# Moving the first norm's statistics to the head of each stage in a fused convolution and feed-forward kernel

## The chip, the cores and the metric

The kernel runs on one core of a Trainium2 chip, in one launch. The core has five engines with queues of their own: TensorE (PE, with its weight loads PEld), VectorE (DVE), ScalarE (ACT), GpSimd (POOL) and SyncE (SP, which here issues nearly all transfers). The metric is the device time of one execution in microseconds; the median of the shown runs is compared. Before the change it is 531.88 us (five runs, 529.43 to 533.68).

## The reference

One block of a diffusion-style network works on 2048 rows (tokens) of 576 channels in bfloat16. Six modulation vectors come from a condition vector. The rows `x` (called `A_q` among the inputs) go through a norm, a gated long convolution and a residual, then through a second norm, a gated feed-forward layer and a second residual.

```
sa, ca, ga, sb, cb, gb = six rows of 576 from silu(c) @ w_mod
h  = layernorm(x) * (1 + ca) + sa
kv = (4-tap shifted sum of k) * v
y  = causal convolution of kv with ssm_k (2048 taps per channel) + kv * ssm_D
x  = x + ga * (h * y)
h  = layernorm(x) * (1 + cb) + sb
x  = x + gb * ((silu(h @ w1) * (h @ w3)) @ w2)     # 576 -> 4608 -> 576
```

The change touches where the statistics of the first `layernorm` are computed, so that line and the product `h * y` are what matters here.

## The kernel before

**Tiling.** The rows are cut into 8 blocks of 256 (two rows to a partition, so a block is a tile of 128 x 2 x 576). The long convolution is done block by block with a short transform: each block of `kv` becomes a spectrum `X` and each block of the filter a spectrum `V`, both by matmuls with a small basis (`L299`, `L313`), which ACT copies out of PSUM (`L302`, `L315`). The spectra are multiplied and summed on DVE (`pair`: `L407`, `L412`, `L414`, 3456 elements to a partition each). `real_parts` (`L516` to `L523`) and `inverse` (PE, `L536`) bring the sum back, ACT copies it to `y` (`L737`), and `residual` (`L550`, `L551`) multiplies by the normed rows `hg` and adds to `x`. Then come the second norm's statistics, its rows `h2row`, a transposition on PE (`L568`) and five ACT instructions that write `h2T` (`L598`), the input of the feed-forward layer.

**The feed-forward layer** runs over 4 row blocks of 512 rows, two convolution blocks each. `stream` makes the hidden part item by item (matmuls `L902` and, for the last 64 channels, `L913`; ACT `sg` L920 and `u` L922; DVE product `h` L924), `down` the second matmul (`L965`) with weights `w2t`. PSUM has four buffers of two banks, shared by the feed-forward items and by the convolution's matmuls.

**Stages.** The convolution of the blocks that row block r + 1 will need is done while row block r is computed. `first_block` does block 0 alone; `conv_second` does block 1 beside the first 12 half-wide items; then `conv(2)` (blocks 2 and 3) runs beside row block 0, `conv(4)` beside row block 1, `conv(6)` beside row block 2. Row block 3 has nothing beside it.

**What sets the order.** The convolution functions are generators. Each `yield` names a cost in us; `advance`, called after each feed-forward item and each chunk of `down`, takes as many steps as their costs allow, so a step's cost moves all that comes after it. `mix` lays steps of a second generator into the gaps that negative costs leave; the four numbers handed to `outcome` are such gaps. The program so written is then put into queues by a scheduler with priorities, which may shift instructions by some places on each engine; where the text below says that one instruction stands behind another, it is by the built programs. Each engine takes its queue in order. `behind(engine)` ties a group to its place after the last instruction so far of that engine.

**The first norm.** `ln_sums` is two ACT instructions for one of a tile's two rows, a sum and a sum of squares (`L442`, output `junk`), `ln_stats` does both rows, and `ln_scales` is six small POOL instructions (`L457` to `L462`), which give scale `l1r` and bias `l1n`. `gate_rows` is two ACT instructions that write the normed rows `hg` (`L497`), and `gate` two DVE instructions that put the modulation on them (`L508`, `L510`). Before the change each block's statistics are taken at one stroke: block 1's at the start of `conv_second`, the first block's of a pair at the head of `conv`, the second block's (`s1`) not until the first block's outcome is under way.

**Loads.** `load_x` brings a block of `x` (288 KB), `load_kv` one of `k` and `v` (720 and 288 KB), `load_k` one of the filter; all are issued by SP in program order among the weights `wst` and `w2t`. `x` has four buffers, `k` and `v` one each.

Of the kernel before, what the change touches and what calls it, by code (L numbers as in the profile page):

```python
# [10 lines left out]
F32 = mybir.dt.float32  # L11
# [4 lines left out]
P = 128  # L16
# [27 lines left out]
class _Kernel:  # L44
    def __init__(self, ctx, tc, q, k, v, shift_k, ssm_k, ssm_D, w1, w3, w2, c, w_mod, out):
        self.tc, self.nc = tc, tc.nc
        self.q, self.k, self.v = q, k, v
        self.shift_k, self.ssm_k, self.ssm_D = shift_k, ssm_k, ssm_D
        self.w1, self.w3, self.w2, self.c, self.w_mod, self.out = w1, w3, w2, c, w_mod, out
        pool = lambda name, **kw: ctx.enter_context(tc.tile_pool(name=name, **kw))  # L50
        self.const = pool("const", bufs=1)
        self.psum = pool("psum", bufs=4, space=bass.MemoryType.PSUM)
        self.dram = pool("spill", bufs=1, space=bass.MemoryType.DRAM)
        self.spec = pool("spec", bufs=4)
        self.wprev = pool("wprev", bufs=2)
        self.prod = pool("prod", bufs=1)
        self.acc = pool("acc", bufs=1)
        self.ld = pool("ld", bufs=1)
        self.kvp = pool("kvp", bufs=1)
        self.x1p = pool("x1p", bufs=4)  # L60
        self.lnp = pool("lnp", bufs=1)
        self.small = pool("small", bufs=4)
        self.hp = pool("hp", bufs=2)
        self.w2p = pool("w2p", bufs=NW2)
        self.xo, self.hg, self.accs = {}, {}, {}
        self.X, self.V, self.Wl = {}, {}, {}
        self.n_w13, self.w13, self.kept = 0, {}, {}

# [415 lines left out]
        return self.tc.issue_after(last)  # L484

    def gate_stats(self, s):
        with self.behind(self.nc.scalar):
            self.l1 = self.ln_stats(self.xo[s], "l1")

    def gate_rows(self, s):  # L490

        x1 = self.xo[s]
        r, b = self.l1
        hg = self.lnp.tile([P, 2, D], BF16, name="hg", tag="hg")
        with self.behind(self.nc.scalar):
            for i in range(2):
                self.nc.scalar.activation(hg[:, i, :], x1[:, i, :], ACT.Identity, bias=b[:, i:i + 1],  # L497
                                          scale=r[:, i:i + 1])
        self.hg[s] = hg
# [267 lines left out]
        self.turned(s, pt, 0, 2)  # L767

    def conv_second(self):
        self.gate_stats(1)  # L770
        yield from self.kv_rows(1)
        yield from self.v_block(1)
        yield from self.pair(self.X[0], self.V[1], 1)
        self.gate_rows(1)
        yield from self.gate(1)
        yield from self.x_spectrum(1)
        self.mod_piece(5)
        self.load_k(2)
        yield from self.x_sums(1)
        yield from self.pair(self.X[1], self.V[0], 1)  # L780
        self.load_kv(2)
        yield from self.outcome(1, self.mix(self.filter_ahead(2)), (3.5, 3.5, 0.0, 2.0), quick=True)
        self.turn_all(1)
        yield 0.0

    def conv(self, s0):
        s1 = s0 + 1
        if s0 == 2:
            self.load_k(s1)
        self.load_x(s0)  # L790
        self.load_x(s1)

        def filters():
            yield from self.k_rows(s1)
            yield -4.0
            yield from self.v_block(s0)
            yield from self.w_spectrum(s1)

        def old():
            V, X = self.old_v(s0 - 1, s0), self.old_x(1, s0)  # L800
            yield from self.pair(X, V, s0)
            for j in range(2, s0):
                X = self.old_x(j, s0)
                yield from self.pair(X, V, s1)
                V = self.old_v(s0 - j, s0)
                yield from self.pair(X, V, s0)
            self.V1 = V
            self.gate_stats(s0)
            yield from self.kv_rows(s0)
            if s0 == 2:  # L810
                yield from self.pair(self.X[0], self.V[s0], s0)
        yield from self.mix(filters(), old())
        self.gate_rows(s0)
        X0, V0 = self.old_x(0, s0), self.old_v(0, s0)

        def beside():
            yield from self.v_block(s1)
            if s0 > 2:
                yield from self.pair(X0, self.V[s0], s0)
            self.X1 = self.old_x(1, s0)  # L820
            yield from self.pair(X0, self.V[s1], s1)
            yield from self.gate(s0)
        yield from self.mix(self.x_spectrum(s0), beside())
        yield from self.x_sums(s0)
        yield from self.pair(self.X[s0], V0, s0)

        def more():
            yield from self.pair(self.X1, self.V[s0], s1)
            yield from self.pair(self.X[s0], self.V1, s1)

        def others():
            self.gate_stats(s1)
            yield from self.kv_rows(s1)
            yield from self.mix(self.x_spectrum(s1), more())
            yield from self.x_sums(s1)
        yield from self.outcome(s0, others(), (5.0, 4.5, 6.0, 0.0), lambda: self.gate_rows(s1))
        yield from self.pair(self.X[s1], V0, s1)
        yield from self.gate(s1)
        ahead = self.mix(self.filter_ahead(s1 + 1)) if s1 + 1 < NBLK else ()
        yield from self.outcome(s1, ahead, (3.5, 3.5, 4.0, 4.0), lambda: self.turn_all(s0))  # L840
        self.turn_all(s1)
        yield 0.0
# [244 lines left out]
```

## Time and profile before

The profiled execution took 533.68 us; its span from the first to the last instruction is 532.0 us, with a mean granted TensorE clock of 0.981.

| engine | busy us | share of the span | instructions |
|---|---|---|---|
| PE | 501.4 | 94% | 3324 |
| PEld | 294.8 | 55% | 3351 |
| DVE | 340.9 | 64% | 515 |
| ACT | 292.8 | 55% | 581 |
| POOL | 71.8 | 13% | 109 |

| stretch of the span, us | what runs |
|---|---|
| 0 to 34 | block 0 alone |
| 34 to 76 | 12 half-wide items, block 1 beside them |
| 76 to 183 | row block 0, blocks 2 and 3 beside it |
| 183 to 303 | row block 1, blocks 4 and 5 beside it |
| 303 to 421 | row block 2, blocks 6 and 7 beside it |
| 421 to 532 | row block 3 |

PE is the busiest engine nearly everywhere, but a share of busy time does not tell where PE waits: for that the stretches and the waits are to be read one by one. In rows of the timeline the first number is the start in us from the span's start, the second how long it lasted, and the square bracket at the end is the engine's idle time before it with what ended it. A row that ends in "x4" merges four instructions in a row.

### The profile page before, as it was taken

Reading aid. Unit: us, or ns where it says so; the run is one execution under the profiler, and the core shown is the slowest. Engines: PE = TensorE matmul, PEld = TensorE weight load, DVE = VectorE, ACT = ScalarE, POOL = GpSimd, SP = SyncE. Lnnn points to the kernel's source line nnn. Section 1 sums busy time; section 2 is a strip of 40 time slices with the busy share of each in tenths; the row PEclk is TensorE's granted clock in tenths of the full one; section 3 lists DMA queues with packets and bytes.
Section 4 is the critical chain, followed back from the end, with each engine's and each line's share of the span. In section 5 each row is a group of like instructions: output and inputs, shape, how many; then the busy total and the mean of one; then the engine's idle time right before and its main releaser. Section 6 shows DMA issues by size and latency. Waiting matters only on the chain.

```text
span 532.0 us, 8687 instructions
## 1 busy us (share of the span) xinstructions
PE 501.4 (94%) x3324; PEld 294.8 (55%) x3351; DVE 340.9 (64%) x515; ACT 292.8 (55%) x581; POOL 71.8 (13%) x109
## 2 busy tenths in 40 slices
PE   7896989997998999999999999999999999999997
PEld 3664865453875743434577643344577644444775
DVE  8897987997992417599997799269772121121011
ACT  6665689558543067757927065776825255455000
POOL 3313001093020000007201000000511000000000
PEclk9988999997997999999999999999999999999999
DMA  8957599673974874378999984464555544541462
GB/s 273 339 163 227 159 287 289 192 256 89 293 229 156 272 264 153 115 229 317 281 350 329 364 254 134 148 200 142 168 157 134 156 128 150 169 127 53 112 174 72
DMA packets 102205, 107.77 MB, mean 203 GB/s; under 512 B 5075, under 2 KB 94228, under 8 KB 102164
## 3 DMA queue, kind: packets, MB, share of 16 engines
q1 hardware_dynamic: 102142, 107.21, 64.4%
q8 instruction: 26, 0.43, 0.3%
q14 instruction: 15, 0.12, 0.1%
q10 hardware_dynamic: 22, 0.01, 0.0%
HBM read 96.00 MB, written 11.21 MB: 202 GB/s over the span
## 4 chain that ended last, share of the span: by engine, by line
PE 66%; DVE 12%; ACT 9%; POOL 5%; DMA 4%; issue 2%; SPq 0%; POOLq 0%; ACTq 0%; DVEq 0%
PE ps L902 35%; PE ps L965 21%; PE ps L913 5%; POOL l1m L457 3%; DVE p L412 3%; DVE z L414 2%; ACT junk L442 2%; DMA wst<-in_B_w_dram 2%; PE ps L313 2%; DVE h L924 1%; ACT h2T L598 1%; DMA V<-Vd 1%; PE ps L536 1%; ACT hg L497 1%; DMA knat<-in_A_ssm_k_dram 1%
## 5 line engine op out<-in xcount | busy, mean ns | idle before, releaser
L902 PE MATMUL ps<-h2T,wst 128*128 128x512 bf16 (+1 forms) x1317 | 267.0, 352 | 5.5 <-DMA wst<-in_B_w_dram 1.9
L902 PEld LDWEIGHTS <-wst 128*128 128x128 bf16 x1344 | 128.6, 99 | 126.9 <-issue 20.8
L920 ACT ACTIVATE sg<-ps 128x512 bf16<-128x512 f32 x144 | 86.3, 599 | 136.7 <-PE ps L913 92.7
L965 PE MATMUL ps<-w2t,h 128*128 128x288 bf16 x1152 | 147.1, 289 | 1.0 <-DMA w2t<-in_B_w_dram 0.8
L965 PEld LDWEIGHTS <-h 128*128 128x128 bf16 x1152 | 113.5, 99 | 31.2 <-issue 1.4
L924 DVE TENSOR_TENSOR h<-sg,u 128x512 bf16<-128x512 bf16 x144 | 60.7, 424 | 95.1 <-ACT u L922 95.0
L922 ACT CAST u<-ps 128x512 bf16<-128x512 f32 x144 | 84.2, 585 | 0.9 <-DVE h L924 0.9
L412 DVE TENSOR_TENSOR p<-X,V 128x3456 bf16<-128x3456 bf16 x28 | 54.8, 1957 | 16.9 <-DMA X<-Xd 11.5
L414 DVE TENSOR_TENSOR z<-z,p 128x3456 bf16<-128x3456 bf16 x28 | 54.8, 1957 | 0.1
L457 POOL TENSOR_SCALAR l1m<-l1s 128x2 f32<-128x2 f32 x7 | 26.3, 3759 | 203.2 <-ACT junk L442 203.2
L913 PE MATMUL ps<-h2T,wst 64*128 64x512 bf16 (+1 forms) x336 | 42.8, 351 | 3.7 <-ACT X L315 3.7
L979 DVE TENSOR_TENSOR og<-ps,gbrow 128x288 bf16<-128x288 f32 x32 | 13.3, 452 | 51.1 <-PE ps L965 51.1
L442 ACT ACTIVATE junk<-x 128x576 bf16<-128x576 bf16 x54 | 37.3, 691 | 0.4
L913 PEld LDWEIGHTS <-wst 64*128 64x128 bf16 x336 | 11.4, 94 | 31.3 <-issue 28.3
L598 ACT ACTIVATE h2T<-ps,sbcol,cbcol 128x256 bf16<-128x256 bf16 x35 | 16.7, 568 | 10.8 <-PE ps L568 10.8
L563 ACT ACTIVATE h2row<-x,l2n,l2r 128x576 bf16<-128x576 bf16 (+1 forms) x24 | 13.7, 642 | 10.7 <-POOL l2n L462 10.7
L335 DVE TENSOR_TENSOR kv<-kv,kvt 128x1152 bf16<-128x1152 bf16 x24 | 18.2, 757 | 0.2
L334 DVE TENSOR_TENSOR kvt<-kh,shk 128x1152 bf16<-128x1152 bf16 x24 | 18.2, 757 | 0.2
L737 ACT CAST y<-ps 128x576 bf16<-128x576 f32 x14 | 8.4, 653 | 16.7 <-PE ps L536 16.7
L315 ACT CAST X<-ps 128x576 bf16<-128x576 f32 x24 | 15.7, 653 | 1.0 <-PE ps L313 1.0
L497 ACT ACTIVATE hg<-x,l1n,l1r 128x576 bf16<-128x576 bf16 x14 | 11.4, 867 | 6.9 <-POOL l1n L462 6.9
L457 POOL TENSOR_SCALAR l2m<-l2s 128x2 f32<-128x2 f32 x6 | 3.5, 579 | 86.0 <-ACT junk L442 86.0
(136 smaller groups left out, 361.2 us busy)
## 6 DMA issues: line engine op xcount, KB each, us to landing
wst<-in_B_w_dram SPq DMA_DIRECT2D x80, 512.0 KB, 4.9
w2t<-in_B_w_dram SPq DMA_DIRECT2D x72, 288.0 KB, 3.8
X<-Xd SPq DMA_DIRECT2D x8, 864.0 KB, 7.6
Xd<-X SPq DMA_DIRECT2D x6, 864.0 KB, 5.2
wst<-in_B_w_dram SPq DMA_DIRECT2D x80, 64.0 KB, 2.2
kh<-in_A_k_dram SPq DMA_DIRECT2D x7, 720.0 KB, 6.0
Vd<-V SPq DMA_DIRECT2D x4, 864.0 KB
V<-Vd SPq DMA_DIRECT2D x4, 864.0 KB, 5.3
```

The costliest lines, as they stand in the source:

```text
L334: nc.vector.tensor_mul(tmp[:], kh[:, 3 - j:5 - j, :], tap(j))
L412: nc.vector.tensor_mul(p[:], X[:], V[:])
L414: nc.vector.tensor_add(z[:], z[:], p[:])
L442: self.nc.scalar.activation(junk[:], src[:, i, :], func, accum_out=out[:, col:col + 1])
L457: e.tensor_single_scalar(mean[:], ssum[:], -1.0 / D, op=ALU.mult)
L598: nc.scalar.activation(dst, src, ACT.Identity, bias=self.sbcol[:, ct:ct + 1], scale=self.cbcol[:, ct:ct + 1])
L902: nc.tensor.matmul(gus[k][:, i, a * n:(a + 1) * n], w[:, 5 * i + ct, (fi + a) * P:(fi + a + 1) * P], hT[:, ct, t0:t1], start=(first and ct ...
L913: nc.tensor.matmul(gus[k][:, i, a * n:(a + 1) * n], w[rows, 4, (fi + a) * P:(fi + a + 1) * P], hT[rows, 4, t0:t1], start=(first and a == 0 ...
L920: nc.scalar.activation(sg[:], gus[k][:, 0, :], ACT.Silu)
L922: nc.scalar.copy(u[:], gus[k][:, 1, :])
L924: nc.vector.tensor_mul(self.h3[:, f:f + m, t0:t1], sg[:].rearrange("p (a t) -> p a t", a=m), u[:].rearrange("p (a t) -> p a t", a=m))
L965: nc.tensor.matmul(acc[t], self.h3[:, f0 + f, t * P:(t + 1) * P], w[:, f, :], start=(f0 + f == 0), stop=(f0 + f == NF - 1))
```

## The change

The statistics are taken row by row, with a cost of 0.8 after each row, and kept in a table by block. In `conv_second` they follow `v_block(1)`, and `gate_rows(1)` and `gate(1)` move from ahead of block 1's spectrum to behind it and behind `mod_piece(5)` (ten matmuls and an ACT copy). In `conv` the second block's statistics move from `others` to just behind `kv_rows(s0)`, so both blocks' statistics stand ahead of `gate_rows(s0)`. The loads of `x` for blocks 2 and 3 move from the head of `conv(2)` into `conv_second`, ahead of `load_kv(2)`, and the first gap of block 1's `outcome` is 5.0 rather than 3.5.

```diff
     def gate_stats(self, s):
-        with self.behind(self.nc.scalar):
-            self.l1 = self.ln_stats(self.xo[s], "l1")
+        ssum, ssq = [self.small.tile([P, 2], F32, name="l1" + k, tag=t) for k, t in (("s", "ssum"), ("q", "ssq"))]
+        for i in range(2):
+            with self.behind(self.nc.scalar):
+                self.ln_sums(self.xo[s], i, ssum, ssq)
+            yield 0.8
+        self.l1[s] = self.ln_scales(ssum, ssq, "l1")
...
     def gate_rows(self, s):
         x1 = self.xo[s]
-        r, b = self.l1
+        r, b = self.l1.pop(s)
...
     def conv_second(self):
-        self.gate_stats(1)
         yield from self.kv_rows(1)
         yield from self.v_block(1)
+        yield from self.gate_stats(1)
         yield from self.pair(self.X[0], self.V[1], 1)
+        yield from self.x_spectrum(1)
+        self.mod_piece(5)
         self.gate_rows(1)
         yield from self.gate(1)
-        yield from self.x_spectrum(1)
-        self.mod_piece(5)
         self.load_k(2)
         yield from self.x_sums(1)
         yield from self.pair(self.X[1], self.V[0], 1)
+        self.load_x(2)
+        self.load_x(3)
         self.load_kv(2)
-        yield from self.outcome(1, self.mix(self.filter_ahead(2)), (3.5, 3.5, 0.0, 2.0), quick=True)
+        yield from self.outcome(1, self.mix(self.filter_ahead(2)), (5.0, 3.5, 0.0, 2.0), quick=True)
...
     def conv(self, s0):
         s1 = s0 + 1
         if s0 == 2:
             self.load_k(s1)
-        self.load_x(s0)
-        self.load_x(s1)
+        else:
+            self.load_x(s0)
+            self.load_x(s1)
...
             self.V1 = V
-            self.gate_stats(s0)
+            yield from self.gate_stats(s0)
             yield from self.kv_rows(s0)
+            yield from self.gate_stats(s1)
             if s0 == 2:
                 yield from self.pair(self.X[0], self.V[s0], s0)
...
         def others():
-            self.gate_stats(s1)
             yield from self.kv_rows(s1)
             yield from self.mix(self.x_spectrum(s1), more())
             yield from self.x_sums(s1)
```

## The prediction

> **What bounds the kernel now.** I read the page's slices first, then busy time by stretches of 10 us, then PE's waits, then the timeline around each. PE is 9.95 of 10 us busy in most stretches; its loss sits in a few places, and there the clock falls too.
>
> ```profile
> 40.00:50.00 10.00, 5.59 (x41) 3.77 (x39) 6.87 (x11) 6.38 (x12) 4.73 (x6) 0.93 0.93 296
> 120.00:130.00 10.00, 6.29 (x23) 2.57 (x21) 6.59 (x11) 8.25 (x18) 4.47 (x10) 0.69 0.21 61
> 160.00:170.00 10.00, 7.87 (x46) 5.46 (x47) 3.56 (x10) 4.67 (x9) 0.73 (x2) 0.66 0.46 149
> 210.00:220.00 10.00, 9.95 (x52) 4.00 (x52) 4.11 (x9) 9.09 (x20) 1.71 (x6) 1.00 0.48 144
> 240.00:250.00 10.00, 9.66 (x52) 4.35 (x52) 9.85 (x12) 8.15 (x18) 8.61 (x3) 1.00 0.94 322
> ```
>
> Columns: PE, PEld, DVE, ACT, POOL busy us (instructions), granted clock, DMA share and GB/s. The clock is halved for 3.41 us from 48.67 and for 6.83 us from 123.76 and from 161.31, each time after a gap in PE; at half rate these cost 1.7, 3.4 and 3.4 us. The middle one has this cause:
>
> ```profile
> 106.85 12.94 POOL L457 TENSOR_SCALAR l1m<-l1s 128x2 f32<-128x2 f32 x1 [23.29 <-ACT junk L442]
> ...
> 119.28 0.44 DVE L924 TENSOR_TENSOR h<-sg,u 128x512 bf16<-128x512 bf16 x1
> ...
> 121.61 1.62 ACT L497 ACTIVATE hg<-x,l1n,l1r 128x576 bf16<-128x576 bf16 x2 [4.32 <-POOL l1n L462]
> ...
> 123.27 0.76 DVE L508 TENSOR_TENSOR hg<-hg,arow 128x1152 bf16<-128x1152 bf16 x1 [3.55 <-ACT hg L497]
> ...
> 124.47 0.61 PE L913 MATMUL ps<-h2T,wst 64*128 64x512 bf16 x2 [3.71 <-ACT X L315]
> ```
>
> Block 3's POOL chain starts at 106.85, while DVE runs without a pause; an instruction that elsewhere takes 0.22 us ends at 119.79, when DVE has run dry (119.72) because it waits for the same rows. ACT's queue stands behind `hg`, so no PSUM buffer comes free and PE stops for 3.71 us. Two other gaps matter:
>
> ```profile
> 43.80 1.63 PE L299 MATMUL ps<-kv,Fb 128*128 128x288 bf16 x12 [2.12 <-DVE kv L337]
> ...
> 47.72 0.65 PE L299 MATMUL ps<-kv,Fb 128*128 128x288 bf16 x4 [2.29 <-ACT u L922]
> ...
> 161.76 0.72 PE L568 MATMUL ps<-ident,h2row 128*128 128x128 bf16 x5 [2.66 <-ACT h2row L563]
> ```
>
> The second is block 1's `hg` blocking ACT's `u`; the third is the end of block 3: DVE is 95 to 100% busy from 90 to 163 but for that one idle of 3.55 us, so this end is set by DVE and the chain behind it.
>
> **Part 1, block 1.** PE's wait of 2.12 stays: `kv` L337 ends at 43.65 in either order. With `hg` behind the four X copies and `gbrow`, the wait of 2.29 shrinks to about 0.4 and the half-clock window goes: some 3.6 us. But DVE then idles from 43.65 to about 48.0, since the X copies stand behind the four L442 (0.82 each, start to start), and the work that it did meanwhile is still to do: from its X sums to block 1's last `h2row` it took 49.89 to 68.87, 19.0 us with 1.1 idle; now 48.0 + 17.9 + five L508/L510/L334/L335-like instructions of 0.75 = 69.7, and 71.3 with the POOL waits and `h` products that fall between. The turn L568 now stands behind the 12th item instead of before it, so its cover is gone: 71.5 + 0.73 + the five `h2T` at 0.47 to 0.57, which the next item consumes one by one, ends that item at 75.8, against 75.4. **+0.4** (-2 to +2): what PE gains first it loses at the turn. The transfers: two `x` of 288 KB now stand on SP ahead of `k`, `v` (both wait for `kv_rows(1)`, to 43.65) and of the next weights (44.12); at 340 GB/s they take 1.7 us of DMA, and those weights, landing 4.9 us after issue, are needed at about 52. Nothing, or up to 1 us if late.
>
> **Part 2, blocks 2 and 3.** ACT is 9.96 of 10 us busy from 80 to 90, and there block 3's four L442 now stand, ahead of `hg` of block 2: 3.3 us. By place: `u` of items 14, 15, 16 come 1.3, 2.2 and 3.4 us later, the last filter copy `Wo` over 4. PE runs out of PSUM buffers at about 84.5 and waits 2.2 us for item 15's. DVE, behind `Wo` and `u`, ends its third L407 (91.91 before) at about 96.4 when one more `h` is taken off: 4.5 late. It had 3.42 us of idle there (before 82.93), which the filter work moved behind block 1 and this lag eat.
>
> POOL's two chains then run in DVE's pauses at 82 to 88 at 0.2 to 0.7 us an instruction, and block 3's `hg` has its scales 35 us early. So DVE gets the 3.55 back: +1.0 at block 3. PE gets its 3.71 and the half-clock back, yet meets DVE earlier: about 3 us at `kv` L337 of block 3 (it waited 1.21 there) and again at block 2's inverse. The end is DVE's. From there, `h2row` of block 3 comes at -0.3 to +1.0, I take **+0.5**. The turn now has 128 matmuls L965 behind it rather than 144: 16 x 0.1225 = **-2.0**. And PE arrives at it about 1.5 us before the rows rather than 2.97 (weight load), so the window at 161.31 should go: **-3.4**. Part 2: -4.9; -1.5 with that window kept.
>
> [...] By this trace a gap of 2.29 us inside one stretch of 3.41 us (45.26 to 48.67) halved the next stretch; 1.96 us of a stretch (41.84 to 45.26) did not. [...] The measured row decides; I take no window at 84.5, by the length nearest to 1.96.
>
> [...]
>
> **Part 3, blocks 4 to 7.** The same four L442 now stand right ahead of `hg` of blocks 4 and 6 (ACT 9.09 of 10 at 210 to 220), two items later than before, by the 0.8 costs. ACT then owes 1.6 for `hg` and 3.3 for the L442; counting PSUM buffers as above PE waits 0.6 + 0.7 = **+1.3** at 222 and about **+1.0** in row block 2, where an X copy falls between. Nothing comes back: block 5's L457 took 7.59 us (240 to 250) and PE was 9.66 busy. Bounds 0 to +2.5 each. DVE's later start (2 to 4 us) is met by PE's turns, which also stand 16 to 32 L965 later.
>
> **Sum.** +0.4 lies inside part 2's absolute times. -4.9 + 1.3 + 1.0 = -2.6 on a span of 532.0, that is 529.4 (533.68 with what lies around it becomes 531.1). The profiled run was the slowest of five; against the median 531.88 - 2.6 = **529.3**.
>
> **Rivals.**
> - *The stall comes back whole* (525.3): ACT's extra work fits into DVE's 3.42 idle, DVE is not late, and the turn comes 3.55 earlier: -3.55 - 2.0 - 3.4 + 2.3 = -6.6. For it: that idle. Against it: ACT at 9.96.
> - *The window at the turn stays* (532.7): -1.5 + 2.3 = +0.8. For it: the turn still waits.
> - *Slower, DVE falls behind at 84 to 92* (535.2): the gap at 84.5 halves the clock, items come at half pace for 3.4 us or more, and DVE's lag is 7 rather than 4.5. With the window at the turn kept: 7 - 4.0 - 2.0 + 2.3 = +3.3. It decides from a lag of 3.7 us with that window, 7.1 without. For it: 2.2 is close to 2.29.
> - *The change does not do what it says* (536.7): DVE pauses too little at 86 to 88, POOL is held until block 3's rows are wanted, and the stall recurs on top of the lag: 4.5 - 2.0 + 2.3 = +4.8. Against it: DVE waits there for `Wo` and `u`.
>
> **How the numbers follow.** Chances: forecast 0.36 (own range 527 to 532), stall back whole 0.18, window stays 0.17, DVE behind 0.21, POOL held 0.08. 0.5% is 2.7 us, about what a measurement of this kernel tells from no change. Faster: 0.18 + 0.6 of 0.36 = 0.40. Slower: 0.29 + a sixth of 0.17 + a little of the forecast's = 0.33. Same 0.27. The range 524.5 to 536.5 leaves out the outer part of the first and last rivals and the bounds of part 3 beyond them.
>
> **What would show it.** Right: block 3's L457 under 1 us near 86; no gap of 3.7 before an L913 near 120; a gap of 2 us near 85 and one of 3 at block 3's L313; the clock at 1.00 from 165 to 180; gaps of about 1 us near 222 and 340. Wrong: a half-clock window after 85, a POOL instruction of over 10 us, or DVE idle between 90 and 160.

## The result, and the profile after

The changed kernel takes 530.62 us in the median of 43 runs (526.96 to 534.76), the kernel before 531.62 us in 80 runs beside it: ratio 0.9985, 95% interval 0.9971 to 0.9999. It is about 1 us faster, less than the 0.5% that the forecast called measurable, where 2.6 us were forecast. Its profiled execution took 529.5 us with a span of 527.4 us and a clock of 0.994; that of before had 533.68, 532.0 and 0.981. So the two spans lie 4.5 us apart and the medians 1.0. Most of what follows is about that difference.

In the changed file the lines below the change stand 5 to 8 further down: L902 is L910, L913 L921, L922 L930, L924 L932, L965 L973, L979 L987, L497 L502, L508 L513, L568 L573.

The same stretches of 10 us (columns: PE, PEld, DVE, ACT, POOL busy us, granted clock, DMA share, GB/s):

```profile
40.00:50.00 10.00, 8.22 (x76) 5.95 (x75) 7.03 (x9) 8.96 (x19) 1.72 (x6) 1.00 1.06 350
80.00:90.00 10.00, 7.98 (x53) 4.29 (x51) 4.72 (x9) 10.00 (x24) 3.81 (x12) 1.00 0.91 298
120.00:130.00 10.00, 9.19 (x69) 5.53 (x66) 9.96 (x16) 9.32 (x21) 3.78 (x6) 1.00 0.44 137
160.00:170.00 10.00, 10.00 (x84) 7.98 (x83) 4.25 (x4) 2.39 (x5) 0.00 (x0) 1.00 0.82 264
210.00:220.00 10.00, 9.04 (x47) 3.80 (x47) 3.92 (x8) 9.62 (x20) 1.71 (x6) 1.00 0.38 117
```

The stall at 120 is gone (PE 9.19 instead of 6.29), and the clock is whole in all five. At 80 to 90 ACT is full and PE at 7.98, which is the price that the forecast named; before, the same stretch reads:

```profile
80.00:90.00 10.00, 9.84 (x70) 5.97 (x71) 6.92 (x13) 9.96 (x22) 1.72 (x6) 1.00 0.84 253
```

From the timeline of the changed kernel:

```profile
84.47 0.22 POOL L457 TENSOR_SCALAR l1m<-l1s 128x2 f32<-128x2 f32 x1 [1.90 <-ACT junk L442]
...
84.91 1.46 PE L910 MATMUL ps<-h2T,wst 128*128 128x512 bf16 x5 [1.89 <-ACT u L930]
...
92.59 1.95 DVE L407 TENSOR_TENSOR z<-X,V 128x3456 bf16<-128x3456 bf16 x1
...
112.34 0.41 PE L313 MATMUL ps<-kv,Fb 128*128 128x288 bf16 x2 [1.56 <-DVE kv L337]
...
122.92 0.76 DVE L513 TENSOR_TENSOR hg<-hg,arow 128x1152 bf16<-128x1152 bf16 x1
...
130.95 1.26 PE L910 MATMUL ps<-h2T,wst 128*128 128x256 bf16 x10 [1.76 <-DMA wst<-in_B_w_dram]
...
158.45 0.56 PE L573 MATMUL ps<-ident,h2row 128*128 128x128 bf16 x5 [0.49 <-ACT h2row L568]
...
159.54 0.56 PE L573 MATMUL ps<-ident,h2row 128*128 128x128 bf16 x5 [0.53 <-ACT h2row L568]
...
216.00 1.24 PE L910 MATMUL ps<-h2T,wst 128*128 128x512 bf16 x4 [0.57 <-ACT u L930]
...
300.90 0.72 PE L366 MATMUL ps<-ident,knat 128*128 128x128 bf16 x10 [1.37 <-DVE og L987]
```

Block 3's POOL chain starts at 84.47 and its first instruction takes 0.22 us instead of 12.94. DVE goes on to block 3's `hg` at 122.92 without idle time. PE waits 1.89 us at 83, and 1.56 for block 3's `kv`. It now also waits 1.76 us for weights at 129, to which it comes earlier than in the forecast's profile. At the turn it waits 0.49 and 0.53, and no half-clock window follows. In the later stages there are new small waits, and one of 1.37 us at the start of row block 2.

### The profile page after: what moved, and what is told of

It is laid out like the page before. It is cut to its first block, busy times and chain, and to the rows that moved or that the text cites. A ratio compares the mean times of both kernels' runs of the same rounds, so it can differ in the third digit from the quotient of the medians.

```text
span 527.4 us, 8683 instructions
## 1 busy us (share of the span) xinstructions
PE 496.5 (94%) x3324; PEld 292.2 (55%) x3351; DVE 341.1 (65%) x515; ACT 293.3 (56%) x581; POOL 45.5 (9%) x109
## 4 chain that ended last, share of the span: by engine, by line
PE 65%; DVE 16%; ACT 9%; DMA 5%; issue 3%; POOL 1%; SPq 0%; POOLq 0%; DVEq 0%; ACTq 0%
PE ps L910 36%; PE ps L973 18%; PE ps L921 5%; DMA wst<-in_B_w_dram 4%; ACT junk L442 3%; DVE p L412 2%; DVE z L414 2%; DVE kv L335 1%; DMA V<-Vd 1%; DVE h L932 1%; DVE kvt L334 1%; PE ps L313 1%; PE ps L541 1%; PE ps L299 1%; ACT sg L928 1%
## 5 line engine op out<-in xcount | busy, mean ns | idle before, releaser
L910 PE MATMUL ps<-h2T,wst 128*128 128x512 bf16 (+1 forms) x1317 | 264.3, 350 | 11.8 <-DMA wst<-in_B_w_dram 4.6
L910 PEld LDWEIGHTS <-wst 128*128 128x128 bf16 x1344 | 128.0, 98 | 132.1 <-issue 22.1
L973 PE MATMUL ps<-w2t,h 128*128 128x288 bf16 x1152 | 145.2, 286 | 1.3 <-DVE og L987 0.8
L973 PEld LDWEIGHTS <-h 128*128 128x128 bf16 x1152 | 112.4, 98 | 30.5 <-issue 1.9
L932 DVE TENSOR_TENSOR h<-sg,u 128x512 bf16<-128x512 bf16 x144 | 60.8, 423 | 100.6 <-ACT u L930 100.5
L930 ACT CAST u<-ps 128x512 bf16<-128x512 f32 x144 | 84.7, 588 | 0.0
L987 DVE TENSOR_TENSOR og<-ps,gbrow 128x288 bf16<-128x288 f32 x32 | 13.2, 452 | 51.3 <-PE ps L973 51.3
L921 PE MATMUL ps<-h2T,wst 64*128 64x512 bf16 (+1 forms) x336 | 42.6, 351 | 0.0
L442 ACT ACTIVATE junk<-x 128x576 bf16<-128x576 bf16 x54 | 37.6, 696 | 0.4
L921 PEld LDWEIGHTS <-wst 64*128 64x128 bf16 x336 | 11.3, 94 | 27.7 <-issue 24.6
L568 ACT ACTIVATE h2row<-x,l2n,l2r 128x576 bf16<-128x576 bf16 (+1 forms) x24 | 13.7, 642 | 12.9 <-POOL l2n L462 12.9
L457 POOL TENSOR_SCALAR l2m<-l2s 128x2 f32<-128x2 f32 x6 | 4.0, 662 | 176.4 <-ACT junk L442 176.4
L407 DVE TENSOR_TENSOR z<-X,V 128x3456 bf16<-128x3456 bf16 x7 | 13.7, 1955 | 0.6 <-DMA X<-Xd 0.6
L541 PE MATMUL ps<-z,Fb 128*128 128x288 bf16 x80 | 11.5, 287 | 2.7 <-DVE z L682 1.5
```

Source lines behind the costliest of these rows:

```text
L442: self.nc.scalar.activation(junk[:], src[:, i, :], func, accum_out=out[:, col:col + 1])
L541: nc.tensor.matmul(ps[:, h, 0:H], self.Fb[:, b, cs], z[:, row, h * H:(h + 1) * H], start=(i == 0), stop=(i == len(terms) - 1))
L910: nc.tensor.matmul(gus[k][:, i, a * n:(a + 1) * n], w[:, 5 * i + ct, (fi + a) * P:(fi + a + 1) * P], hT[:, ct, t0:t1], start=(first and ct ...
L921: nc.tensor.matmul(gus[k][:, i, a * n:(a + 1) * n], w[rows, 4, (fi + a) * P:(fi + a + 1) * P], hT[rows, 4, t0:t1], start=(first and a == 0 ...
L930: nc.scalar.copy(u[:], gus[k][:, 1, :])
L932: nc.vector.tensor_mul(self.h3[:, f:f + m, t0:t1], sg[:].rearrange("p (a t) -> p a t", a=m), u[:].rearrange("p (a t) -> p a t", a=m))
```

## The experiments

Each ratio is against runs of before on the same chip; us are the ratio times 532.

**The parts, alone and together.** First only `conv_second` and `conv(2)` as changed (`gate_stats_once` takes the statistics at one stroke, as before). The edit is against the changed kernel and in short form:

```diff
-            yield from self.gate_stats(s0)
+            if s0 > 2: self.gate_stats_once(s0)
+            else: yield from self.gate_stats(s0)
             yield from self.kv_rows(s0)
-            yield from self.gate_stats(s1)
+            if s0 == 2: yield from self.gate_stats(s1)
...
         def others():
+            if s0 > 2: self.gate_stats_once(s1)
```

> The change in conv_second and conv(2) alone; conv(4) and conv(6) take their statistics as before. Theory A (the later stages cost what the profile of after shows, 1.8 + 1.4 us, because the second block's L442 stand ahead of hg on ACT): 3.2 us below after, 527.4, and the gaps near 215 and 350 go. Rival B (those two differences are chance, of where the half-clock windows fall): as after, 530.6, within 0.7.

Measured: 0.9922 (0.9903 to 0.9941), -4.1 us. Its counterpart has the same switch turned round, and `conv_second` as before:

> The counterpart: conv_second and conv(2) as before, only conv(4) and conv(6) take both blocks' statistics at the head. Theory A: 3.2 us above before, 534.8. Rival B: as before, 531.6, within 0.7.

Measured: 1.0039 (1.0018 to 1.0061), +2.1. Then block 1's part alone, and `conv(2)` alone:

> Only block 1's part: statistics behind v_block(1), hg behind the spectrum, the loads of x earlier, 5.0 for 3.5. All conv stages as before. The forecast's part 1 (gain at the front given back at the turn): +0.4, 532.0. Rival (the half-clock window near 48 is in most executions of before and goes): -1.7 to -2.5, 529.1 to 529.9. Block 3's POOL chain is held as before in either case (an instruction of over 10 us near 105, a PE gap of over 3 us near 120).

Measured: 0.9988 (0.9962 to 1.0014), -0.6; POOL held for 14.00 us and a PE gap of 3.71 at 121.5, as expected of it.

> Only conv(2): both blocks' statistics at its head, row by row; block 1 and the later stages as before. Theory A (early POOL chain frees block 3's rows, the stall of 3.55 us goes, paid for by ACT near 84): -3 to -5, 527 to 529. Rival (DVE's lag of the forecast, 4.5 us, eats the stall, and windows at half clock are as frequent as before): 0 to -1, 530.6 to 531.6. POOL instructions of block 3 near 86 under 1 us in either case.

Measured: 0.9917 (0.9891 to 0.9943), -4.4. Next the changed kernel again, and the changed kernel with block 1's part taken back:

> The changed kernel once more, beside the others on one chip. If the parts add up (-0.6, -4.4 and +2.1 us from the runs of each part alone): ratio 0.995, 2.9 us below before. If the later stages cost more with the first ones in place (3.6 us between the profiles of after and of the first two stages alone, 2.2 between those of the last two alone and before): ratio 0.998 to 0.999, 0.5 to 1 us below before. In its profile PE's wait at the turn of row block 2 (near 299, 1.4 us behind DVE's og L987, after a transfer of V) is at 0.3 to 0.5 if that was chance, over 1 if not.

Measured: 0.9983 (0.9963 to 1.0003), -0.9, which confirms the first result. PE's wait at the start of row block 2 was 0.79.

> The changed kernel with block 1's part taken back: statistics of block 1 first, hg ahead of the spectrum, 3.5 for 5.0, the loads of x at the head of conv(2). If block 1's part is worth nothing: as after on the same chip, within 1 us. If it costs what the forecast gave it or more (its turn's cover is gone, and the weights' transfers stand behind two loads of x): 1 to 1.5 us below after. If the half-clock window near 48 was worth 1.7 in most executions: 1.5 above after.

Measured: 0.9967 (0.9951 to 0.9984), -1.8. So block 1's part is worth -0.6, +0.3 or +0.9 us, according to what it is added to, nothing that can be told from zero; `conv(2)` -3.5 to -4.4; the later stages +2.1, +2.6 or +3.2. The two later stages take back half or more of what the earlier one brings.

**Later stages.** Five profiles are of kernels with the change there (the fifth is the changed kernel with its turn filled, further down). In them row block 1 takes 121.5 or 121.6 us, against 119.4 to 120.7 without the change; row block 2 takes 117.9 to 119.5 against 117.5 to 118.0. The rows that answer to the forecast's place, from the timeline of the kernel with only the last two stages changed:

```profile
223.11 0.40 PE L313 MATMUL ps<-kv,Fb 128*128 128x288 bf16 x2 [0.34 <-ACT X L315]
224.08 1.89 PE L917 MATMUL ps<-h2T,wst 128*128 128x512 bf16 x8 [0.57 <-ACT u L937]
...
307.94 0.72 PE L366 MATMUL ps<-ident,knat 128*128 128x128 bf16 x10 [0.32 <-DVE og L994]
```

The 0.34 and 0.57 are in each of the five. The third row is the place where the first profile of after has 1.37 us: PE waits there for DVE's `og`, which stands behind a product that waits for a `V` from DRAM (5.12 us there). In the five profiles this wait is 0, 0.32, 0.79, 1.37 and 1.56 us, and 0.44 in the profile of before. That part varies from execution to execution, and much of row block 2's time with it.

**Does the place ahead of `hg` matter?** Block 3's statistics one step later, behind `hg` of block 2, the later stages as before:

```diff
             yield from self.kv_rows(s0)
-            yield from self.gate_stats(s1)
...
         def beside():
+            if s0 == 2: yield from self.gate_stats(s1)
             yield from self.v_block(s1)
```

> The first two stages changed, conv(4) and conv(6) as before, and block 3's statistics one step later: ACT takes them behind hg of block 2, so that POOL's chain for block 3 starts near 92, where DVE has begun to run without a pause. If POOL is held whenever DVE runs large products back to back: an instruction of over 5 us, scales of block 3 late, and with them hg near 121: the stall comes back, ratio 0.997 to 1.000. Rival (a POOL chain among DVE instructions of 0.75 us and under takes 1 to 2 us an instruction and has 28 us of time): no stall, and ACT's queue lighter at 80 to 84, ratio 0.989 to 0.992.

Measured: 0.9869 (0.9839 to 0.9899), -7.0, with six runs, and again:

> Block 3's statistics behind hg of block 2 with block 1's part changed, the later stages as before, once more: 0.986 to 0.990 if the first result (0.9869 from few runs) holds.

Measured: 0.9892 (0.9861 to 0.9922), -5.7, again with six. This order beats both kernels. W and Wo reach DVE sooner and PE's wait of 1.9 near 83 is gone (0.7, 0.4 and 0.6 remain at 77, 80 and 90). The POOL chain, in the timeline of the first of the two:

```profile
87.38 2.47 POOL L457 TENSOR_SCALAR l1m<-l1s 128x2 f32<-128x2 f32 x1 [5.95 <-ACT junk L442]
87.49 1.95 DVE L407 TENSOR_TENSOR z<-X,V 128x3456 bf16<-128x3456 bf16 x1
89.36 0.42 DVE L943 TENSOR_TENSOR h<-sg,u 128x512 bf16<-128x512 bf16 x1
...
90.46 0.43 DVE L943 TENSOR_TENSOR h<-sg,u 128x512 bf16<-128x512 bf16 x1 [0.69 <-ACT u L941]
```

L457 ends at 89.85, just after DVE has run dry at 89.77. A hold of over 5 us was expected by one theory; DVE did not, as I had written, run without a pause there, so this run does not refute it. The same order in all three stages, and that one move alone on the kernel before:

> The changed kernel, but in all three stages the second block's statistics stand behind hg of the first block rather than ahead of it. If the cost of the later stages comes from ACT's extra 3.3 us right ahead of hg (PE's waits for X and u near 215 and 255): row block 1's hidden part falls back from 79.46 to about 78.7 us, and the total is that of the kernel with this order in conv(2) alone, ratio 0.986 to 0.990. If it comes from where DVE's work and the transfers of V fall (og late near 280 and 300): 2 to 2.5 us more than that, 0.990 to 0.994.

Measured: 0.9916 (0.9889 to 0.9943), -4.5. Row blocks 1 and 2 take 121.38 and 118.60 us: the cost stays, and PE's wait near 214 is 0.92 in one piece. So by the profile it does not come from standing right ahead of `hg`, as the forecast had it. The runs alone do not settle that: 0.9916 and the 0.9892 of the same chip lie within their intervals.

> The kernel before with one move: block 3's statistics from the second block's outcome to behind hg of block 2, in conv(2) alone; block 1, the loads and the later stages as before. If the place of these four L442 is what matters: ratio 0.986 to 0.989, as with block 1's part changed too. If block 1's part and the earlier loads of x are needed for it: 0.990 to 0.993.

Measured: 0.9931 (0.9905 to 0.9956), -3.7. That is no better than the -4.4 of `conv(2)` alone, which has block 1 as before too and takes block 3's statistics ahead of `hg`. So the place behind `hg` shows a gain only where block 1's part is changed as well (-7.0 and -5.7 against -4.1), and why it should need that part is not shown. A third place, which moves block 2's statistics to block 1's turn, where ACT idles:

```diff
         self.turn_all(1)
+        self.gate_stats_once(2)
...
-            yield from self.gate_stats(s0)
+            yield from self.gate_stats(s1)
             yield from self.kv_rows(s0)
-            yield from self.gate_stats(s1)
```

> The first two stages changed, conv(4) and conv(6) as before, and block 2's four L442 moved on to block 1's turn, where ACT idles 2.8 us behind h2T; block 3's stand where block 2's stood. If ACT's queue at 76 to 87 sets DVE's work there (DVE waits 2.80, 1.87 and 0.78 us for u and Wo, and runs without a pause after that to the end of block 3): PE's wait of 1.9 near 82.7 falls under 0.8 and block 3's end comes 1.5 to 3 us earlier; 1 to 2.5 us below the first two stages alone, ratio 0.987 to 0.990. Rival (the weights' transfers or the turn's own chain set the end): ratio 0.992 as with the first two stages alone.

Measured: 0.9953 (0.9932 to 0.9974), -2.5: slower than with the first two stages alone, not faster. Instead of one wait near 83 PE has three between 76 and 79 (0.84, 0.31 and 0.80, for `kT` and W), because ACT now comes late to `sg` and `kT`, and DVE still idles before 82:

```profile
82.18 0.43 DVE L942 TENSOR_TENSOR h<-sg,u 128x512 bf16<-128x512 bf16 x1 [3.41 <-ACT u L940]
```

The loss does not come from these waits, though. Block 3's second five transposes start 127.7 us into the stage, as with the first two stages alone (127.8). But this kernel has 144 matmuls of `down` behind that point again, not 128, and from there to row block 1 it takes 19.7 instead of 17.6 us, with one half-clock window of 3.41 us in both.

**Is it POOL that makes the rows late?** The kernel before, with block 3's scales taken from POOL. Only the six scale instructions of block 3 move, to DVE, and there the inverse root is replaced by its first Newton step, 1.5 - 0.5 var, so these scales are approximate:

```diff
-            self.l1 = self.ln_stats(self.xo[s], "l1")
+            self.l1 = self.ln_stats(self.xo[s], "l1", self.nc.vector if s == 3 else None)
...
-        e = self.nc.gpsimd
+        e = engine or self.nc.gpsimd
...
-        e.tensor_tensor(rstd[:], var[:], self.neghalf[:, 0:n], op=ALU.pow)
+        if engine is None: e.tensor_tensor(rstd[:], var[:], self.neghalf[:, 0:n], op=ALU.pow)
+        else: e.tensor_scalar(rstd[:], var[:], -0.5, 1.5, op0=ALU.mult, op1=ALU.add)
```

> [...] If POOL's hold by DVE is what makes hg of block 3 late: no DVE idle of 3.55 us near 123, no PE gap of 3.7 near 121, block 3's end 2.5 to 3.5 us earlier; 3 to 4.5 us below before, ratio 0.992 to 0.994, although the four L442 stand as late as ever. Rival (hg is late because ACT comes to the L442 late, or because of what stands before it on ACT): the stall stays, ratio 0.999 to 1.001.

Measured: 0.9972 (0.9957 to 0.9987), -1.5. In its profile the stall is gone, with the statistics as late as ever: DVE runs on to `hg` at 121.17 with no idle time, and no half-clock window lies at 110 to 119, which matters further down. That POOL is what held the rows is shown. But the gain is half of the least that was expected of it. PE came to block 3's turn early:

```profile
159.97 0.71 PE L571 MATMUL ps<-ident,h2row 128*128 128x128 bf16 x5 [4.09 <-ACT h2row L566]
```

The wait is 4.09 instead of 2.66 us, and a half-clock window of 6.83 us begins in it, at 158.97. Part of what the stall took is given back at the turn, which here still has 144 matmuls behind it.

**What is the window at the turn worth?** PE's wait there is filled with matmuls of no use, in before (13 of them), in after and in the best order (9 each):

```diff
+        if s1 == 3: self.warm(13)
         self.turn_all(s1)
```

> The kernel before with 13 matmuls of 128x512 of no use (2.8 us) right ahead of block 3's transposes, where PE waits 2.66 us for the rows. If the window at that turn costs the median execution what the forecast took off for it (3.4 us): ratio 0.993 to 0.995. If it costs about 1 to 1.5 us in the mean: 0.997 to 0.998. Over 1.000 if the filled matmuls delay the transposes more than the clock gives.

Measured: 0.9989 (0.9969 to 1.0008), -0.6. In its profile no window is left at the turn: behind it 17 matmuls of `down` take 2.25 us from 163.92.

> The changed kernel with 9 such matmuls (1.9 us) at the same place, where its PE waits 0.5 to 1.4 us. If the change has taken the window away as forecast: no gain, or a loss of up to 1 us, ratio 0.998 to 1.000. If the window stays in part of the executions: 0.5 to 1 us less than the changed kernel, ratio 0.996 to 0.998.

Measured: 0.9961 (0.9937 to 0.9985), about -1.2 against the changed kernel on another chip (0.9983), which is within the two intervals.

> Block 3's statistics behind hg of block 2 (ratio 0.987 and 0.989 so far) with 9 such matmuls at the turn, where PE waits 1.6 to 1.9 us: 0.984 to 0.988 if a window follows that wait in about half of the executions; 0.988 to 0.990 if it does not matter.

Measured: 0.9895 (0.9867 to 0.9923), no gain over 0.9869 and 0.9892. Taking away PE's wait at the turn is nowhere worth 3.4 us. The profile of the first of these three held a surprise: it had no stall at 120 either. So the kernel before was profiled again.

**Before, profiled three more times.**

> The kernel before once more, one look. If its half-clock windows are the same in each execution: 3.41 us after 48.7, 6.83 after 123.8 and 6.83 after 161.3. If they lie by chance against the gaps: other places or lengths, with the same gaps of 2.3, 3.7 and 2.7 us in PE and the same POOL instruction of about 13 us.

It took 528.56 us, with a span of 526.9. The windows lie elsewhere (3.41 us from 110.88 and from 158.66), as the second of these expects; but the gap of 3.7 and the hold of 13 us, which both expect, are not there. Two rows of its stretches, columns as above, and its timeline:

```profile
110.00:120.00 10.00, 8.79 (x46) 4.91 (x47) 8.80 (x11) 5.05 (x9) 7.92 (x6) 0.83 0.70 221
120.00:130.00 10.00, 8.44 (x63) 4.88 (x60) 9.97 (x17) 9.24 (x22) 3.70 (x6) 1.00 0.47 139
```

```profile
105.04 9.73 POOL L457 TENSOR_SCALAR l1m<-l1s 128x2 f32<-128x2 f32 x1 [22.08 <-ACT junk L442]
...
111.21 0.66 PE L313 MATMUL ps<-kv,Fb 128*128 128x288 bf16 x2 [2.41 <-DVE kv L337]
111.66 3.09 PE L902 MATMUL ps<-h2T,wst 128*128 128x256 bf16 x15
...
113.95 0.75 DVE L551 TENSOR_TENSOR x<-x,hg 128x1152 bf16<-128x1152 bf16 x1
...
115.89 0.43 DVE L924 TENSOR_TENSOR h<-sg,u 128x512 bf16<-128x512 bf16 x1 [1.20 <-ACT u L922]
...
120.31 0.75 DVE L508 TENSOR_TENSOR hg<-hg,arow 128x1152 bf16<-128x1152 bf16 x1
```

Here PE waits 2.41 us for `kv`; a half-clock window runs from 110.88 to 114.29; 15 matmuls take 3.09 us, `u` is late, and DVE runs dry for 1.20 us at 114.69. POOL's instruction ends in that pause, at 114.77. `hg` of block 3 is then ready in time: L508 has no idle time before it. The two other profiles:

> The kernel before, a third look. If a half-clock window behind PE's wait for kv (L337, near 109) is what frees POOL: either a window lies at 109 to 117, DVE idles 1 us or more near 116, the L457 of block 3 is held under 11 us and there is no PE gap of 3.7 near 120; or no window lies there, L457 is held about 13 us and the gap of 3.7 is there. Rival (the two are not connected): a stall with that window, or no stall without it.

> The kernel before, a fourth look, with the same two outcomes. The stage from the first half-wide item to the next row block takes about 150 us with the stall and about 146 without.

Both had the second outcome (534.35 and 532.48 us): no window there, holds of 14.12 and 13.11 us, and the stall. From the third profile of before:

```profile
105.83 14.12 POOL L457 TENSOR_SCALAR l1m<-l1s 128x2 f32<-128x2 f32 x1 [22.09 <-ACT junk L442]
...
123.43 0.76 DVE L508 TENSOR_TENSOR hg<-hg,arow 128x1152 bf16<-128x1152 bf16 x1 [3.56 <-ACT hg L497]
...
124.64 0.61 PE L913 MATMUL ps<-h2T,wst 64*128 64x512 bf16 x2 [3.72 <-ACT X L315]
```

Of the seven profiles of kernels that have `conv(2)` and its POOL chain as before, five have the stall and no window at 110 to 119, and two have such a window (110.88 and 115.56) and no stall. How often the timed runs have it is not known.

## Why the prediction was wrong

It had the direction and the parts, and missed the size: 2.6 us forecast, 1.0 measured. From the first L902 of the stage to the first of row block 1, with the point in it where block 3's second five transposes start:

| profile | stage | to the transposes | from there on | row block 1 | row block 2 |
|---|---|---|---|---|---|
| before, of the forecast | 150.5 | 130.0 | 20.5 | 119.7 | 117.8 |
| before, second | 145.7 | 126.4 | 19.3 | 119.4 | 117.9 |
| before, third | 151.1 | 130.6 | 20.5 | 120.2 | 117.9 |
| before, fourth | 149.2 | 130.0 | 19.2 | 120.1 | 118.0 |
| before, turn filled | 147.0 | 129.0 | 18.0 | 119.7 | 117.8 |
| after | 143.4 | 127.3 | 16.1 | 121.5 | 119.3 |
| after, again | 145.7 | 127.9 | 17.7 | 121.5 | 118.7 |
| after, block 1 as before | 143.2 | 127.2 | 16.1 | 121.6 | 119.5 |
| first two stages alone | 145.4 | 127.8 | 17.6 | 119.4 | 117.8 |
| `conv(2)` alone | 145.6 | 128.0 | 17.6 | 120.4 | 117.9 |
| block 2 at block 1's turn | 147.4 | 127.7 | 19.7 | 119.8 | 117.8 |
| block 3 behind `hg` | 140.0 | 123.9 | 16.1 | 120.1 | 117.8 |
| block 3 behind `hg`, again | 145.3 | 127.5 | 17.7 | 120.0 | 117.8 |

The last two rows are one program, 5.2 us apart in this stage. The spans of the four profiles of before are 532.0, 526.9, 532.6 and 530.8 us, 530.6 in the mean; those of the two of after 527.4 and 530.3, 528.9 in the mean. The forecast stood on one of the longer ones, and took what it saw there for what every execution has.

**The step that failed: Part 2's -3.4 for the half-clock window at the turn.** The column "from there on" measures it. With 128 matmuls behind the turn it is 16.1 us without a window and 17.6 or 17.7 with one of 3.41 us. With 144 it is 18.0 without a window (before, turn filled) and 19.2 to 20.5 in the four profiles of before. So the window costs 2.5, 1.3, 2.4 and 1.1 us before, 1.8 in the mean, and 0, 1.6, 0, 1.6 and 1.6 us in the five changed profiles, 0.9 in the mean. The change takes off 0.9 and not 3.4.

Three things were wrong in that term. It counted 6.83 us at half rate, though the window began while PE still waited: even in the forecast's own profile it cost about 2.5. It took that execution for all of them, where the mean of four is 1.8. And it took a wait of about 1.5 us for harmless, because 1.96 us of idle time had been in one stretch; three of the five changed profiles keep a window. The second profile of after shows how:

```profile
160.21 0.56 PE L573 MATMUL ps<-ident,h2row 128*128 128x128 bf16 x5 [1.36 <-ACT h2row L568]
161.30 0.62 PE L573 MATMUL ps<-ident,h2row 128*128 128x128 bf16 x5 [0.53 <-ACT h2row L568]
```

One stretch, from 158.19, holds both waits, 1.88 us of idle time, and the next one is at half clock; the forecast did not count the second wait. The filled turn agrees: before, filling the wait brings the runs -0.6 us (-1.6 to +0.4).

**The end of block 3: +0.5 forecast.** The column "to the transposes" gives 127.6 in the mean of the five changed profiles against 129.3 in the four of before, -1.6, and -2.6 against the three that have the stall. The lag was too large: DVE's third L407 ends at 94.54, not at about 96.4, which is 2.6 us late and not 4.5. DVE's idle time near 84 is 5.45 us (2.80, 1.87 and 0.78) against 3.42. From 40 to 160 DVE idles 9.6 instead of 12.4 us in these two profiles, and the turn comes 2.8 us earlier in the stage. But in the profile of before without the stall the end of block 3 lies at 126.4, before that of any of the five: there was nothing to win in such an execution. This error of 2.1 made good most of the 2.5 lost at the window: -1.6 - 2.0 - 0.9 = -4.5 for the stage, where -4.9 was forecast. That this sum came out nearly right is luck: two errors of opposite sign.

**The 16 matmuls fewer behind the turn, -2.0:** right. Without a window at the turn it takes 18.0 us with 144 and 16.1 with 128; with one of 3.41 us, 19.7 and 17.6.

**Part 1:** forecast as nothing outside part 2; -0.6 to +0.9 measured. The wait of 2.29 at 45 is gone and waits of 0.62 and 0.65 stand at block 1's turn, as it said. The weights were late at 53 by 0.93, within its bound of 1.

**Part 3:** forecast +2.3. By the profiles +1.6 and +0.9, by runs +2.1 to +3.2. The size is right or a little small, and the place half right: 0.34 + 0.57 at 215 for the 1.3 near 222, 0.49 at 350 for the 1.0. The rest comes later, in the second matmul (42.2 or 42.3 instead of 40.8 to 41.2 us in row block 1), in waits for `X`, for `og` and at the next row block's start. Its mechanism is not settled: with the L442 behind `hg` the cost was the same.

**The list of what would show it.** L457 under 1 us near 86: yes, 0.22 at 84.5. No gap of 3.7 near 120: yes. A gap of 2 near 85: 1.89. One of 3 at block 3's L313: no, 1.56. Full clock from 165: yes. None of the signs of a wrong forecast appeared in that profile. The first of them, a window after 85, is in the profile of the first two stages alone (from 84.87); its 127.8 us to the transposes are still among the others' 127.2 to 128.0. One profile of after could not have shown the error: half of it lay in the profile of before, and the window that stays is in some executions only.

**The clock in the timed runs.** Each timed run has its span and its mean granted clock on record. One minus the clock, times the span, is an estimate of what half rate took from it, as if PE had been busy all the time. On one chip it is 7.9 us in the mean of 51 runs of before and 6.2 in 22 of the changed kernel: -1.7 (plus or minus 1.0, at 95%). The rest of the time moves by +0.6 (plus or minus 0.7). The forecast's profile has 10.1 us by the same measure, more than the mean execution. With the first two stages alone the clock's part falls by 2.8 (plus or minus 0.9) and the rest by 1.5 (0.6). With the last two alone the clock's part does not move (-0.1, plus or minus 0.8) and the rest grows by 2.4 (0.8). So more than half of what the first stages bring is clock, and what the later ones cost is not.

**What remains.** The stages by profiles give -4.5 + 1.6 + 0.9 = -2.0 us, the two mean spans -1.7, the medians -1.0 and -0.9 with intervals of -1.5 to -0.1 and -2.0 to +0.2. By the runs of the parts, Parts 1 and 2 bring -4.1 where -4.9 was forecast, and the later stages cost 3.1 on top of them (-1.0 against -4.1) where 2.3 was forecast. Each of these two distances of 0.8 is within what the runs can tell, so how the miss of 1.6 is shared between the parts stays open. What the profiles do show is the mis-sized term inside Part 2.

## What to carry to other kernels

Before a stall or a clock window is taken off the time, look whether a second execution of the same kernel has it: one profile is one draw, and a wait that ends in a chance pause of another engine was there in five of the seven profiles that could have it and not in two. Where a statistic is moved early, more than one place should be tried: with block 1's part changed, the same four instructions of ACT were worth -4.1 us ahead of `hg` and -5.7 to -7.0 behind it, and with block 1 as before -4.4 and -3.7, which cannot be told apart. And a gain found in one stage is not to be copied to the next: there POOL was held for 7.59 us as well, with PE 9.66 of 10 us busy beside it, and the same move cost 2 to 3 us.

## What the runs showed of the hardware

**When a held L457 ended.** In the profile of before, 340 of the 514 steps from one DVE instruction to the next overlap: the next starts 0.07 to 0.11 us before the one ahead ends. Each L457 held for over 7 us ended when this chain first broke, be it by 0.03 us. From the timeline of the kernel with the first two stages alone:

```profile
235.40 7.59 POOL L457 TENSOR_SCALAR l1m<-l1s 128x2 f32<-128x2 f32 x1 [27.14 <-ACT junk L442]
...
242.15 0.77 DVE L559 TENSOR_TENSOR hg<-hg,y 128x1152 bf16<-128x1152 bf16 x1
242.95 0.76 DVE L560 TENSOR_TENSOR x<-x,hg 128x1152 bf16<-128x1152 bf16 x1
```

L560 needs L559's result and starts 0.03 us after its end, not before it; POOL is done at 242.99. All 21 instructions L457 held for over 7 us in these profiles end 0.075 to 0.082 us after the first such seam. In the forecast's profile the 12.94 us span 14 instructions of DVE and end at 119.79, 0.08 us after DVE has run dry; the 7.59 from 241.24 end 0.08 us after L550, behind which L551 starts with a seam of 0.03. Shorter holds do not all follow this: the 1.93 us from 152.94 in the profile of after end with one DVE instruction and no seam, and so does the 0.57 at 126.33 in that of before, with DVE as busy. What holds POOL is not shown beyond these times.

**Which idle time a half clock followed.** In these profiles the granted clock fell to 0.50 for stretches of 3.41 us or two of them in a row, and their grid differs between profiles: such a stretch starts at 48.67 in the first profile of before and at 110.88 in the second. The stretches around the three windows of the first, from 41.84 on:

| stretch, us | granted clock | PE idle, us | clock of the next stretch |
|---|---|---|---|
| 41.84 to 45.26 | 1.00 | 1.96 | 1.00 |
| 45.26 to 48.67 | 1.00 | 2.29 | 0.50 |
| 48.67 to 52.08 | 0.50 | 0.00 | 1.00 |
| 120.35 to 123.76 | 1.00 | 3.00 | 0.50 |
| 123.76 to 127.18 | 0.50 | 0.71 | 0.50 |
| 127.18 to 130.59 | 0.50 | 0.00 | 1.00 |
| 157.90 to 161.31 | 1.00 | 2.21 | 0.50 |
| 161.31 to 164.73 | 0.50 | 0.82 | 0.50 |
| 164.73 to 168.13 | 0.50 | 0.00 | 1.00 |

Counted so over PE's idle time in all 20 profiles, from 38 us on, a stretch at full clock with 1.97 us or more of idle time was followed by one at half clock in 20 of 20 cases; with 1.49 to 1.96 in 12 of 40; with less, never. A stretch already at half clock was followed by another in 8 of 8 cases with 0.71 us or more of idle time, and by full clock in 32 of 32 with 0.53 or less; so windows of 3.41 and of 6.83 us were seen behind the same gap. The gap of 1.89 us near 83 is in six profiles. The clock halved behind it in one of them (84.87, first two stages alone), where one stretch held 1.97 us of idle time, and stayed whole in the other five, where a stretch held 1.95 us or less. So in these profiles the same gap had a window behind it in one execution and none in another: a gap just under 2 us had a chance of costing clock, not a price.
